# Cluster-routed attention with a SoLU feed-forward: cluster maxima in PSUM, fewer idle products, a shorter centroid norm and a new instruction order

## The chip, the cores and the metric

The kernel runs on one core of a Trainium2 chip. The metric is device time in microseconds (us) of one execution; lower is better. Five engines work side by side, each in its own program order: TensorE (PE in the profile, PEld its weight loads), VectorE (DVE), ScalarE (ACT), GpSimd (POOL) and SyncE (SP), which only issues DMAs here. They wait for each other through semaphores.

## The reference

```python
q_assign = argmax(einsum('bhsd,hcd->bhsc', q_n, c_n))     # 16 centroids a head
k_assign = argmax(einsum('bhsd,hcd->bhsc', k_n, c_n))
mask = q_assign[:, :, :, None] == k_assign[:, :, None, :]
scores = where(mask, scale * q @ k.T, -1e9)
attn = softmax(scores) @ v                                 # 4 batches, 8 heads, 768 x 64
x = attn.transpose(0, 2, 1, 3).reshape(3072, 512)
h = x @ w_in                                               # 512 -> 1024
solu = h * softmax(h)
ln = (solu - mean) / sqrt(var + 1e-6) * g_ln
return ln @ w_out                                          # 1024 -> 512, fp32
```

A query attends only to keys of its own cluster. The norm of a query or key does not change its argmax, so only the centroids are normalised.

## The kernel before, in words

The mask is made part of the score product. For every token a one-hot row of 32 values says which centroid is nearest, and it is written below the 64 rows of q and k in the operands `qbig` and `kbig`. One product over 80 or 96 rows then gives the scaled score plus a large constant where the clusters agree, and the exponential takes the constant off again, so that masked pairs come out as nothing.

The work is cut into named pieces. A table `ORDER` (names only) fixes in what order the pieces are recorded; `Weave.run` calls them one after the other, and each engine executes its own pieces in that order. A second table, `AWAY`, moves a named piece to another engine than its default. The list of needs that `add` is given (`needs`, `after`) is only checked against `ORDER`; the semaphores come from the tiles that the instructions really touch. The names used below, with the line of the profile of the kernel before:

- `S r.x` (L641): half a region of scores on TensorE, two 256-column products into a score bank pair `sb`; a region is 1024 columns. `E r` (L651): its exponential on ScalarE, 144 in all, 36 a batch.
- `V n.j` (L663): the values, six 65-column products into the one PSUM bank `ob`, of which they use the first 432 of 512 columns. `N g` (L675 reciprocal, L686 product) on VectorE normalises a group of up to six such results out of `ob`; then `ob` may be written again.
- The assignment, eleven items (`0.0`, `0.0.1`, `0.1` ... `3.2`), two pairs of heads each from batch 1 on: `cl` (L470) multiplies q and k by the centroids, `tb` (L479) transposes the result back to SBUF (`cst`), `mx` (L489) takes the maximum over the 16 centroids, `oh` (L493) compares with it and writes the one-hot rows, `ot` (L500, L505) transposes them, `pl` (L529, L531) places them in `qbig` and `kbig`. `ca` (L437, L439, L441) casts the transposed q and k, `xt` transposes them, `cv` (L554, L556) casts v.
- Batch 0 gets its q and k transposed by TensorE (`tp`, L396, fp32) with a copy out of PSUM (`xa`, `xt` with a bank, L407, L409); later batches by VectorE (L421).
- The feed-forward of 24 token tiles `f`: `h f.f2.part` (L772) and `hm` (L782), `ex` (L798), `u` (L805), `bn` (L816), `y` (L844) and its scaling `sc` (L856 on ScalarE, L858 on VectorE), `ou` the store. `wi` casts w_in (L580), `me`, `mf`, `ce` centre w_out.
- At the start, while the first DMA is under way: `wu`, idle products on TensorE (L946), and the norm of the centroids `cx`, `cy`, `cz` (L908 to L922).

The maximum lives in a small SBUF tile `mx`, and the comparison reads it broadcast over the 16 centroids:

```python
asg[t, "mx"] = pr.tile([P, 2 * HALF // NC_], F32, name="mx")
nc.vector.reduce_max(asg[t, "mx"][:, :wide(t) // NC_], each(asg[t, "cst"], t), axis=AX)
```

Of the kernel before, what the change touches and what calls it, by code (L numbers as in the profile page):

```python
# [20 lines left out]
    ca0.0.1.1.0 ca0.2.0.1 ca1.0.0.1 ca3.1.1.0 ca3.2.0.1 cv0.0.1 cv0.1.0 cv0.2.1 cv1.2.0  # L21
    cv1.3.1 cv2.0.1 cv2.1.0 cv3.0.0 cv3.0.1 cv3.3.0 pl0.0.0.1 pl0.0.1.0 pl0.1.1.1 pl2.2.1.0
    xa0.0.0 xa0.1.0 xa0.1.1 xa0.2.0 xa0.2.1 xa0.3.0 xt0.1.0 xt0.1.1 xt0.2.0 xt0.3.0
""".split(), "ACT"))
AWAY.update(dict.fromkeys("""
    as0 as11 as14 as15 as17 as18 as19 as2 as22 as23 as4 as5 as9 bl1.2 bl3.0 ce0 ce2 ce4 km mk
    pl0.0.1.0.0 pl0.1.0.0 pl0.1.0.1 pl0.2.0.0 pl0.2.1.0 pl0.3.0.0 pl0.3.1.1 pl1.0.0.0
    pl1.2.0.0 pl2.0.0.0 pl2.0.0.1 pl2.0.1.1 pl2.2.0.0 pl3.0.0.1 pl3.2.0.1 pl3.2.1.0 sc0 sc1
    sc12 sc13 sc14 sc16 sc4 sc9
""".split(), "DVE"))  # L30
AWAY.update(dict.fromkeys("""
    ca0.0.0.0.0 ca0.0.0.0.1 ca0.0.0.1.0 ca0.0.0.1.1 ce1 ce3 pl0.0.1.1 u0.0 u1.0 u10.0 u11.0
    u12.0 u13.0 u15.0 u16.0 u17.0 u18.0 u19.0 u2.0 u21.0 u22.0 u3.0 u4.0 u5.0 u6.0 u7.0 u8.0
    u9.0
# [4 lines left out]
lc ld0.0.0.0 ld0.0.1.0 ld0.0.0 ld0.0.1 ld0.1.0 ld0.1.1 lv0.0 ld0.2.0 ld0.2.1 ld0.3.0 lo3 lv0.1  # L39
ld0.3.1 lg lv0.2 lo1 lo2 lo0 cx z5 cy cz wu tp0.0.0.0 tp0.0.0.1 tp0.0.1.0 tp0.0.1.1 cp xa0.0.0  # L40
xt0.0.0 xa0.0.1 xt0.0.1 tp0.1.0.0 xa0.1.0 cb cl0.0 tb0.0 mx0.0 oh0.0 ot0.0 ca0.0.0.0.0 z3
ca0.0.1.0.0 ca0.0.0.0.1 cc ca0.0.0.1.1 ca0.0.0.1.0 pl0.0.1.1 pl0.0.0.0 ca0.0.1.0.1 ca0.0.1.1.1
ca0.0.1.1.0 tp0.1.0.1 tp0.1.1.0 xt0.1.0 xa0.1.1 cl0.0.1 tp0.1.1.1 cv0.0.1 xt0.1.1 pl0.0.0.1
tp0.2.0.0 tp0.2.0.1 tb0.0.1 mx0.0.1 oh0.0.1 ot0.0.1 pl0.0.1.0.1 pl0.0.1.0.0 pl0.0.1.1.1 cl0.1 sg
pl0.0.1.1.0 z1 ca0.1.1.0 cv0.0.0 ca0.1.0.0 xa0.2.0 pl0.0.1.0 tp0.2.1.0 xt0.2.0 xa0.2.1 S0.0 S0.1
E0 tp0.2.1.1 xt0.2.1 S1.0 tp0.3.0.0 S1.1 S2.0 S2.1 tp0.3.0.1 tb0.1 mx0.1 oh0.1 xa0.3.0 E1 E2 cl0.2
xt0.3.0 S3.0 S3.1 V0.0 V0.1 V1.0 S4.0 S4.1 V1.1 tp0.3.1.0 tb0.2 E3 S5.0 S5.1 E4 E5 ot0.1 N0 mx0.2
gt tp0.3.1.1 S6.0 S6.1 V2.0 V2.1 S7.0 S7.1 V3.0 V3.1 xa0.3.1 gk xt0.3.1 cl0.3 E6 E7 cv0.1.0
pl0.1.1.1 ca0.1.0.1 ca0.3.0.0 pl0.1.1.0 ca0.3.0.1 z2 ca0.1.1.1 oh0.2 pl0.1.0.0 pl0.1.0.1 gw S8.0
S8.1 S9.0 S9.1 me0 me1 ot0.2 tb0.3 pl0.2.1.0 N1 pl0.2.0.0 mx0.3 mk oh0.3 ca0.2.0.0 ca0.2.1.0  # L50
ca0.3.1.0 ca0.2.1.1 pl0.2.1.1 pl0.2.0.1 E8 E9 ca0.2.0.1 S10.0 S10.1 S11.0 S11.1 V4.0 V4.1 V5.0
V5.1 E10 S12.0 S12.1 cv0.2.1 E11 E12 mf N2 ot0.3 pl0.3.0.0 ld1.0.0.0 li0 ld1.0.0.1 ld1.0.0.2
ld1.0.0 ld1.0.1.0 lv0.3 ld1.0.1.1 ld1.0.1.2 ld1.0.1 cv0.1.1 ca0.3.1.1 pl0.3.1.0 pl0.3.0.1 cv0.2.0
cv0.3.0 cv0.3.1 wi0 S13.0 S13.1 V6.0 V6.1 S14.0 S14.1 V7.0 V7.1 pl0.3.1.1 N3 km ce0 E13 E14 S15.0
S15.1 S16.0 S16.1 E15 E16 V8.0 V8.1 S17.0 S17.1 E17 V9.0 V9.1 S18.0 S18.1 E18 S19.0 S19.1 N4 ce5
V10.0 V10.1 V11.0 V11.1 S20.0 S20.1 E19 S21.0 S21.1 E20 E21 li1 li3 N5 V12.0 V12.1 ptx0 S22.0
S22.1 V13.0 V13.1 li2 xt1.0.0 xt1.0.1 tx0 xt1.1.0 xt1.1.1 ld1.2.0.0 ld1.2.0.1 ld1.2.0.2 ld1.2.0
ld1.2.1.0 ld1.2.1.1 ld1.2.1.2 ld1.2.1 S23.0 S23.1 cl1.0 E22 E23 S24.0 S24.1 E24 S25.0 S25.1 E25
ca1.0.0.1 cl1.1 N6 tb1.0 tb1.1 mx1.0 ce6 ce1 ca1.0.1.0 wi1 wi3 wi2 z4 ca1.1.0.0 ca1.0.1.1
ca1.1.1.0 ca1.0.0.0 S26.0 V14.0 V14.1 S26.1 S27.0 V15.0 S27.1 V15.1 h0.0.0 h0.0.1 N7 E26 E27 S28.0  # L60
S28.1 E28 V16.0 V16.1 V17.0 S29.0 S29.1 h0.1.0 V17.1 S30.0 S30.1 E29 E30 oh1.0 hm0.0 N8 ot1.0 ce2
pl1.0.1.0 pl1.0.0.1 pl1.0.1.1 bl1.0 ce3 lv1.0 tx2 lv1.1 lv1.2 ld2.0.0.0 ld2.0.0.1 ld2.0.0.2 h0.1.1
S31.0 S31.1 V18.0 V18.1 V19.0 S32.0 S32.1 V19.1 h1.0.0 N9 hm0.1 pl1.0.0.0 xt1.2.0 E31 S33.0 S33.1
E32 E33 h1.0.1 S34.0 S34.1 V20.0 V20.1 V21.0 S35.0 S35.1 V21.1 h1.1.0 E34 E35 S36.0 S36.1 N10
hm1.0 xt1.2.1 h1.1.1 S37.0 S37.1 V22.0 V22.1 V23.0 E36 E37 S38.0 S38.1 E38 V23.1 cl1.2 N11 tb1.2
ce4 hm1.1 ex0.0 cv1.0.0 cv1.0.1 u0.0 ca1.1.0.1 S39.0 S39.1 S40.0 S40.1 V24.0 V24.1 h2.0.0 h2.0.1
V25.0 xt1.3.0 E39 E40 ex1.0 h2.1.0 h2.1.1 S41.0 S41.1 S42.0 hm2.0 h3.0.0 S42.1 V25.1 xt1.3.1 hm2.1
V26.0 V26.1 h3.0.1 E41 cl1.3 S43.0 as0 bn0.0 N12 tb1.3 mx1.2 oh1.2 bn0.1 E42 S43.1 S44.0 S44.1
V27.0 ex2.0 E43 E44 V27.1 h3.1.0 h3.1.1 V28.0 S45.0 S45.1 S46.0 S46.1 V28.1 V29.0 E45 E46 tu0
V29.1 y0.0 S47.0 S47.1 y0.1 N13 cv1.1.0 ca1.2.0.0 u1.0 ca1.2.1.0 ca1.1.1.1 cv1.1.1 ca1.3.0.1 as1  # L70
ca1.2.0.1 bn1.0 hm3.0 ot1.2 ce7 S48.0 S48.1 y0.2 V30.0 E47 E48 S49.0 S49.1 E49 tx4 ld2.0.0
ld2.0.1.0 tu1 ld2.0.1.1 ld2.0.1.2 ld2.0.1 lv1.3 ld2.2.0.0 ld2.2.0.1 ld2.2.0.2 V30.1 V31.0 V31.1
S50.0 S50.1 h4.0.0 S51.0 S51.1 E50 E51 V32.0 V32.1 y0.3 S52.0 S52.1 bn1.1 hm3.1 ag0 N14 pl1.2.0.0
pl1.2.0.1 pl1.2.1.1 pl1.2.1.0 h4.0.1 as2 bl1.2 hm4.0 ag1 al0 u2.0 ca1.2.1.1 S53.0 S53.1 V33.0
# [99 lines left out]
def kernel(  # L174
# [737 lines left out]
    def norm_2():  # L912
        nc.gpsimd.tensor_tensor(c_s0[:], c_nsq[:], halves[:, 0:1], op=Alu.pow)
# [441 lines left out]
```

## Time and profile before

| | before |
|---|---|
| time, median of 3 runs | 221.88 us (221.68 to 222.42) |
| span of the profiled execution, first to last instruction | 220.5 us |
| PE busy | 211.4 us, 96% |
| ACT busy | 192.8 us, 87% |
| DVE busy | 185.7 us, 84% |
| POOL busy | 158.8 us, 72% |
| granted TensorE clock | 1.000 |

The profiled execution has a span and no time of its own in the records; the median of the runs stands 1.4 us above its span. Busy times are sums of instruction durations; an engine's share says nothing yet of which one is waited for. In rows of groups, the columns are line, engine, operation, output <- input, partitions x elements and type, count, then busy us, mean ns of one, and the idle time just before them with what ended it. In rows of waits they are engine, tile and line, what was waited for, total us, times, longest.

### The profile page before, as it was taken

What the parts mean: (1) busy time and instruction counts of PE and PEld (TensorE: products, weight loads), DVE (VectorE), ACT (ScalarE), POOL (GpSimd) and SP (SyncE); (2) the same over time, 40 slices, a digit from 0 to 9 for tenths busy, and PEclk for the clock granted to TensorE, in tenths of its full rate; (3) what the DMA queues carried; (4) which work ended last, traced back from release to release, by engine and by line L of the source; (5) the groups of instructions that cost most, each with busy time, mean ns of one, the idle gap of its engine ahead of it and who ended that gap; (6) DMA issues with size and microseconds to landing.
All of it is one profiled execution on the core that took longest, in us unless ns stands there. A gap on an engine that the chain in (4) does not pass through costs nothing.

```text
span 220.5 us, 6292 instructions
## 1 busy us (share of the span) xinstructions
PE 211.4 (96%) x2401; PEld 148.9 (68%) x2431; DVE 185.7 (84%) x430; ACT 192.8 (87%) x245; POOL 158.8 (72%) x198
## 2 busy tenths in 40 slices
PE   7899999999999999999999999999999999999984
PEld 4567577677678776777677677666777767655442
DVE  3699979968999999896799999994888856989982
ACT  3799999999999998999999989999999888685362
POOL 3686969897898999549939997879889054456610
PEclk9999999999999999999999999999999999999999
DMA  5998999999999993999999981939584229777522
GB/s 199 394 402 259 189 175 300 126 154 259 164 154 169 190 188 62 174 248 210 153 225 162 180 184 38 171 92 209 151 173 90 72 64 168 154 120 170 163 94 100
DMA packets 120911, 38.33 MB, mean 174 GB/s; under 512 B 109993, under 2 KB 116401, under 8 KB 120881
## 3 DMA queue, kind: packets, MB, share of 16 engines
q1 hardware_dynamic: 120448, 37.40, 81.7%
q10 hardware_dynamic: 432, 0.52, 0.7%
q8 instruction: 19, 0.31, 0.6%
q14 instruction: 12, 0.09, 0.2%
HBM read 23.11 MB, written 6.29 MB: 133 GB/s over the span
## 4 chain that ended last, share of the span: by engine, by line
PE 72%; DVE 10%; DMA 6%; POOL 5%; issue 3%; ACT 2%; SPq 1%; DVEq 0%; ACTq 0%; POOLq 0%
PE sb L641 22%; PE hb L772 16%; PE mb L844 15%; PE ob L663 12%; DMA w_st<-in_moe_w_in_dram 4%; PE hb L470 3%; DMA raw<-in_q_dram 2%; DVE w_st L782 2%; PE hb L396 2%; DVE xt L421 2%; DVE bs L816 2%; POOL kbig L441 1%; PE mb L470 1%; POOL w_in_sb L580 1%; POOL v L556 1%
## 5 line engine op out<-in xcount | busy, mean ns | idle before, releaser
L651 ACT ACTIVATE e<-sb 128x1024 bf16<-128x1024 f32 x144 | 139.9, 1024 | 8.9 <-PE sb L641 8.1
L641 PE MATMUL sb<-qbig,kbig 80*128 80x256 bf16 (+3 forms) x648 | 83.8, 261 | 1.3 <-ACT e L651 1.0
L641 PEld LDWEIGHTS <-kbig 80*128 80x128 bf16 (+1 forms) x648 | 62.9, 119 | 25.4 <-issue 8.6
L805 POOL TENSOR_TENSOR u<-e_sb,w_st 128x1024 bf16<-128x1024 bf16 x21 | 45.1, 2145 | 20.0 <-ACT e_sb L798 13.3
L663 PEld LDWEIGHTS <-e 128*128 128x128 bf16 x1152 | 48.6, 97 | 10.4 <-DVE x L686 0.6
L663 PE MATMUL ob<-v,e 128*128 128x65 bf16 x1140 | 51.4, 193 | 0.2
L772 PE MATMUL hb<-w_in_sb,xT 128*128 128x512 bf16 x173 | 50.6, 379 | 0.9 <-POOL v L1323 0.3
L844 PE MATMUL mb<-w_out_c,uT 128*128 128x512 bf16 x165 | 45.5, 379 | 1.2 <-DVE y L858 0.4
L816 DVE BATCH_NORM_STATS2 bs<-u 128x6 f32<-128x512 bf16 x48 | 31.6, 680 | 1.1 <-POOL u L805 1.1
L798 ACT ACTIVATE e_sb<-w_st,nmax 128x1024 bf16<-128x1024 f32 (+1 forms) x25 | 27.8, 1113 | 3.2 <-DVE w_st L782 1.8
L439 POOL CAST qbig<-xt 64x768 bf16<-64x768 f32 (+1 forms) x31 | 25.7, 830 | 6.5 <-PE ob L663 2.7
L441 POOL TENSOR_SCALAR kbig<-xt 64x768 bf16<-64x768 f32 (+1 forms) x32 | 27.6, 865 | 2.4 <-DVE xt L409 0.8
L840 POOL TENSOR_TENSOR alpha<-var,halves 128x1 f32<-128x1 f32 x24 | 15.3, 638 | 12.6 <-DVE var L823 8.0
L421 DVE STREAM_TRANSPOSE xt<-raw 128x768 f32<-128x768 f32 x24 | 22.5, 959 | 0.1
L844 PEld LDWEIGHTS <-uT 128*128 128x128 bf16 x176 | 15.2, 97 | 10.2 <-issue 0.8
L772 PEld LDWEIGHTS <-xT 128*128 128x128 bf16 x192 | 15.8, 98 | 8.8 <-issue 0.6
L686 DVE TENSOR_TENSOR x<-ob,den 128x256 bf16<-128x256 f32 (+2 forms) x40 | 19.0, 474 | 1.4
L782 DVE TENSOR_SCALAR_CACHE_REDUCE w_st<-hb 128x512 f32<-128x512 f32 x24 | 16.3, 680 | 3.8 <-PE hb L772 3.7
L782 DVE TENSOR_SCALAR_CACHE_REDUCE w_st<-hb,nmax 128x512 f32<-128x512 f32 x24 | 17.8, 740 | 1.9 <-PE hb L772 1.5
L856 ACT ACTIVATE y<-mb,alpha 128x512 f32<-128x512 f32 x15 | 10.3, 685 | 6.5 <-POOL alpha L840 3.6
L675 DVE RECIPROCAL den<-ob 128x4 f32<-128x4 f32 (+2 forms) x40 | 7.1, 178 | 10.4 <-PE ob L663 10.1
L556 POOL CAST v<-vf 128x384 bf16<-128x384 f32 x22 | 10.9, 504 | 3.3 <-DMA vf<-in_v_dram 2.6
(109 smaller groups left out, 202.6 us busy)
## 6 DMA issues: line engine op xcount, KB each, us to landing
vf<-in_v_dram SPq DMA_DIRECT2D x16, 384.0 KB, 5.3
out_dram<-y SPq DMA_DIRECT2D x23, 256.0 KB, 2.5
raw<-in_k_dram SPq DMA_DIRECT2D x26, 192.0 KB, 4.6
raw<-in_q_dram SPq DMA_DIRECT2D x24, 192.0 KB, 5.1
w_g<-in_moe_w_out_dram SPq DMA_DIRECT2D x4, 512.0 KB, 8.7
w_st<-in_moe_w_in_dram SPq DMA_DIRECT2D x4, 512.0 KB, 8.0
raw<-in_q_dram SPq DMA_DIRECT2D x3, 384.0 KB, 6.6
raw<-in_k_dram SPq DMA_DIRECT2D x3, 384.0 KB, 7.6
```

What stands on the lines that cost most here:

```text
L421: nc.vector.transpose(xts[b, p, i][:], raw_of(b, p, i))
L439: (nc.vector if e == "DVE" else nc.gpsimd).tensor_copy(dst, src)
L441: (nc.vector if e == "DVE" else nc.gpsimd).tensor_scalar(dst, src, scalar1=inv_C, scalar2=1.0, op0=Alu.mult, op1=Alu.mult)
L641: nc.tensor.matmul(reg[:, c:c + wd], kb[u, pp, side_of(h), keys], qb[u, pp, side_of(h), su * P:su * P + wd])
L651: nc.scalar.activation(es[r][:, :w], src, Act.Exp, scale=exp_scale, bias=-exp_scale)
L663: nc.tensor.matmul(ops_of(group_of[n])[:, s, :VW], es[r][:, c0:c0 + P], v1[index[b, pair_of(h)] % R][:, side_of(h), kt, :VW], start=(kt == ...
L772: nc.tensor.matmul(hb[f2][:], xTs[f][:, dc, :], w_in_sb[:, dc, f2 * BANK:(f2 + 1) * BANK], start=(dc == 0), stop=(dc == n_dc - 1))
L782: nc.vector.tensor_scalar(ff[f, "h"][:, f2 * BANK:(f2 + 1) * BANK], hb[f2][:], scalar1=-1.0, scalar2=nmax[:, f2 - 1:f2] if f2 else 3.0e38, ...
L798: nc.scalar.activation(ff[f, "e"][:, cols(f, f2)], ff[f, "h"][:, cols(f, f2)], Act.Exp, bias=ff[f, "nmax"][:, n_ff2 - 1:], scale=-1.0, acc ...
L805: (nc.vector if e == "DVE" else nc.gpsimd).tensor_tensor(ff[f, "u"][:, cols(f, f2)], ff[f, "e"][:, cols(f, f2)], ff[f, "h"][:, cols(f, f2) ...
L816: nc.vector.bn_stats(ff[f, "bs"][:, f2, :], ff[f, "u"][:, f2 * BANK:(f2 + 1) * BANK])
L844: nc.tensor.matmul(y_of(f, x), ff[f, "uT"][:, fc, :], w_out_c[:, fc, parts_of(f, x)], start=(fc == 0), stop=(fc == n_fc - 1))
```

## The change

It has five parts.

1. The maxima are written to `ob`, columns 432 up to 480, where no value is written, in place of the SBUF tile. There is one such place, so a maximum now also comes after the comparison of the item before.
2. `wu` issues five idle products for seven. Three short ones of 256 columns, `wx0` to `wx2`, stand later: two among the transposes of batch 0, one at the very end.
3. The norm of the centroids has one VectorE instruction less; GpSimd adds the small constant instead, in a spare column of `upper`.
4. `AWAY` is new. VectorE loses the nine one-hot placings that it had from batch 1 on (seven into `qbig`, two into `kbig`), which go to GpSimd, and gains four `y` scalings from ScalarE. ScalarE loses early v casts, copies of transposes and q or k casts. GpSimd gains the nine placings, some early v casts and one step of the w_out centring, and gives up one `u` and one `wi`.
5. `ORDER` is written anew from the first name to the last.

```diff
+    def highest(t):
+        return ob[:, 6 * VS:6 * VS + wide(t) // NC_]
+
     def assign_max(t):
-        asg[t, "mx"] = pr.tile([P, 2 * HALF // NC_], F32, name="mx")
-        nc.vector.reduce_max(asg[t, "mx"][:, :wide(t) // NC_], each(asg[t, "cst"], t), axis=AX)
+        nc.vector.reduce_max(highest(t), each(asg[t, "cst"], t), axis=AX)

     def assign_hot(t):
         asg[t, "oh"] = pr.tile([P, 2 * HALF], BF16, name="oh")
         nc.vector.tensor_tensor(each(asg[t, "oh"], t), each(asg[t, "cst"], t),
-                                asg[t, "mx"][:, :wide(t) // NC_].unsqueeze(2)
+                                highest(t).unsqueeze(2)
                                 .to_broadcast([P, wide(t) // NC_, NC_]), op=Alu.is_ge)
...
     def norm_2():
         nc.gpsimd.tensor_tensor(c_s0[:], c_nsq[:], halves[:, 0:1], op=Alu.pow)
+        nc.gpsimd.tensor_scalar(c_s1[:], c_s0[:], scalar1=2e-6, scalar2=1.0, op0=Alu.add,
+                                op1=Alu.mult)

     def norm_3():
         nc.vector.reciprocal(c_r0[:], c_s0[:])
-        nc.vector.tensor_scalar(c_r0[:], c_r0[:], scalar1=c_nsq[:], scalar2=c_s0[:],
-                                op0=Alu.mult, op1=Alu.add)
-        nc.vector.tensor_scalar(c_norm[:], c_r0[:], scalar1=0.5, scalar2=1e-6,
+        nc.vector.tensor_scalar(c_norm[:], c_r0[:], scalar1=c_nsq[:], scalar2=c_s1[:],
                                 op0=Alu.mult, op1=Alu.add)
...
-        for _ in range(7):
+        for _ in range(5):
             nc.tensor.matmul(sb[0][:, 0], idle[:, :P], idle)

+    def idle_product():
+        nc.tensor.matmul(sb[0][:, 0, :2 * P], idle[:, :P], idle[:, :2 * P])
...
-        add(f"mx{tm}", "DVE", ..., tbs, [f"mx{item_name(t - 1)}"] if t else [])
+        add(f"mx{tm}", "DVE", ..., tbs + ([f"oh{item_name(t - 1)}"] if t else ["xa0.0.1"]))
...
 ORDER = """
-V41.0 V41.1 y2.0 mx2.0 as4 N17 E63 ... V42.0 V42.1 S68.0 S68.1 V43.0 V43.1 sc2 oh2.0 ot2.0 N18 pl2.0.1.1
+V41.0 V41.1 S64.1 ex4.0 y1.1 E63 mx2.0 S65.0 S65.1 y1.2 cv1.3.0 E64 N17 ... V42.0 cv1.3.1 V42.1 oh2.0 V43.0 E66
```

Two places show what moves. The first is item 2.0 of the assignment. On VectorE, before, from its maximum to its comparison and its transpose (`mx` and `cst` are SBUF tiles, `den` and `x` belong to the normalisations `N17` and `N18`):

```order
L489 TENSOR_REDUCE mx<-cst 128x48 [waits DVE_49]
L835 TENSOR_SCALAR es_1699<-esum 128x1 [waits Activation_49]
L675 RECIPROCAL den<-ob 128x6 [waits PE_49]
L686 TENSOR_TENSOR x<-ob,den 128x6x64 [waits DVE_49]
L493 TENSOR_TENSOR oh<-cst,mx 128x768
L500 STREAM_TRANSPOSE oht<-oh 128x768 [waits DVE_49]
L675 RECIPROCAL den<-ob 128x4 [waits PE_49]
```

The same stretch of VectorE after the change:

```order
L489 TENSOR_REDUCE ob<-cst 128x48 [waits DVE_49,PE_49]
L675 RECIPROCAL den<-ob 128x6 [waits DVE_49]
L686 TENSOR_TENSOR x<-ob,den 128x6x64 [waits DVE_49]
L493 TENSOR_TENSOR oh<-cst,ob 128x768 [waits PE_49]
L858 TENSOR_SCALAR y<-mb,alpha 128x512 [waits Pool_49]
L675 RECIPROCAL den<-ob 128x4 [waits PE_49]
```

The maximum and the comparison have each got a wait for TensorE that they had not: the maximum for the last product of V41.1, the comparison for the last product of V42.1, both in `ob`. The normalisation no longer waits for TensorE itself, since the maximum ahead of it has.

On TensorE after the change, the end of V42.1 and the start of V43.0 (`e` is the exponential's tile as weight, `v_1` the values):

```order
L663 LDWEIGHTS e
L663 MATMUL ob<-v_1_103,e 128x65
L663 LDWEIGHTS e
L663 MATMUL ob<-v_1_103,e 128x65
L663 LDWEIGHTS e [waits DVE_49]
L663 MATMUL ob<-v_1_103,e 128x65 [waits Pool_49]
L663 LDWEIGHTS e
```

The weight load with the wait is the first of V43.0, and the instruction that it waits for is the comparison of item 2.0. Nothing else of TensorE stands between V42.1, for which that comparison waits, and this load. In the kernel before, no wait of TensorE is for L489 or L493.

The second place is item 1.0, on VectorE after the change (`N8` is the pair with `den` and `x`):

```order
L476 STREAM_TRANSPOSE cst<-hb_93 128x384 [waits PE_49]
L489 TENSOR_REDUCE ob<-cst 128x48 [waits DVE_49,PE_49]
L675 RECIPROCAL den<-ob 128x4 [waits DVE_49]
L686 TENSOR_TENSOR x<-ob,den 128x2x2x64 [waits DVE_49]
L493 TENSOR_TENSOR oh<-cst,ob 128x768
```

and before:

```order
L479 STREAM_TRANSPOSE cst<-hb_93 128x384 [waits PE_49]
L489 TENSOR_REDUCE mx<-cst 128x48 [waits DVE_49]
L675 RECIPROCAL den<-ob 128x4 [waits PE_49]
L686 TENSOR_TENSOR x<-ob,den 128x2x2x64 [waits DVE_49]
L493 TENSOR_TENSOR oh<-cst,mx 128x768
```

After the change the maximum waits for V17.1, the normalisation and the comparison stand behind it, and V18.0 on TensorE waits for that comparison. Between V17.1 and V18.0 TensorE has S30.0, S30.1 and h0.0.0.

More of the change, by code (lines that the diff above doesn't have):

```diff
@@ L135 @@
-bn19.1 bn20.0 bn20.1 N39 hm22.0 as19 ag19 as20 as21 al19 E143 y18.0 y18.1 y18.2 y18.3 h22.1.0
-ptx23.0 h22.1.1 V95.0 ou16 sc18 V95.1 hm22.1 N40 tx23.0 ag20 tu19 y19.0 y19.1 y19.2 ptx23.1 y19.3
-tu20 ou17 tu21 ou18 ex22.0 h23.0.0 h23.1.0 tx23.1 as22 bn21.0 bn21.1 ag21 u22.0 al20 sc19 h23.0.1
-y20.0 y20.1 y20.2 y20.3 sc20 hm23.0 bn22.0 h23.1.1 ptu22.0 ptu22.1 bn22.1 hm23.1 tu22.1 tu22.0
-ex23.0 ex23.1 ou19 y21.0 y21.1 y21.2 y21.3 ou20 u23.0 u23.1 ag22 as23 ptu23.0 ptu23.1 tu23.1
-bn23.0 bn23.1 ag23 al21 sc21 ou21 tu23.0 y22.0 y22.1 y22.2 y22.3 y23.1.0 y23.1.1 y23.1.2 y23.1.3
@@ new lines @@
+V94.1 E143 h22.0.1 h22.1.0 as20 sc17 tu20 y18.0 y18.1 bn20.0 ex21.0 bn20.1 ag20 y18.2 y18.3 al18
+N39 h22.1.1 al19 sc18 ptx23.0 u21.0 hm22.0 hm22.1 V95.0 ou17 V95.1 y19.0 ou18 y19.1 al20 as21 y19.2
+N40 y19.3 ex22.0 tx23.0 h23.0.0 ptx23.1 bn21.0 h23.1.0 sc19 tx23.1 h23.0.1 h23.1.1 hm23.0 y20.0
+hm23.1 bn21.1 y20.1 y20.2 y20.3 sc20 tu21 u22.0 ex23.0 ag21 ex23.1 bn22.0 al21 ptu22.0 ptu22.1
+bn22.1 y21.0 tu22.0 tu22.1 y21.1 y21.2 as22 u23.0 y21.3 ptu23.0 as23 ou19 sc21 u23.1 bn23.0 ou20
+ptu23.1 y22.0 y22.1 y22.2 ag22 y22.3 tu23.0 tu23.1 y23.0.0 al22 y23.1.0 y23.0.1 bn23.1 y23.1.1 ag23
@@ L891 @@
     c_bd = const.tile([P, n_pair, 2 * NC_], F32, name="c_bd")
[L894 removed]
+    upper = const.tile([P, 120], F32, name="upper")
+    upper, c_s1 = upper[:, :2], upper[:, 2:3]
     nc.gpsimd.memset(upper[:], 0.0)
```

218 lines of the change are left out of this document (108 added, 110 removed).

## The prediction

> **What bounds the kernel now.** I read the page's busy times first, then its time slices, then each engine's busy time in stretches of the span, then the list of waits, and the timeline at the places of the change.
>
> ```profile
> PE 211.4 (96%) x2401; PEld 148.9 (68%) x2431; DVE 185.7 (84%) x430; ACT 192.8 (87%) x245; POOL 158.8 (72%) x198
> PEclk9999999999999999999999999999999999999999
> ```
>
> TensorE is busy 96% of the span, at the full granted clock in every slice. The span is 220.5 us, so what can be gained without taking work from TensorE is 220.5 - 211.4 = 9.1 us and no more. The stretches say where that idle time lies; the columns are the stretch, its length, then busy time of PE, PEld, DVE, ACT and POOL.
>
> ```profile
> 0.00:10.00 10.00, 8.34 (x48) 4.81 (x48) 4.21 (x19) 4.94 (x10) 4.74 (x21) 1.00 0.79 285
> ...
> 10.00:50.00 40.00, 38.26 (x499) 27.40 (x501) 34.90 (x75) 39.02 (x49) 33.01 (x47) 1.00 1.01 233
> 50.00:85.00 35.00, 34.73 (x435) 26.11 (x436) 33.33 (x73) 34.34 (x42) 31.22 (x35) 1.00 1.02 178
> 90.00:200.00 110.00, 108.93 (x1267) 78.14 (x1285) 93.02 (x218) 100.13 (x125) 76.54 (x82) 1.00 0.79 151
> 210.00:215.00 5.00, 4.39 (x32) 2.19 (x31) 4.37 (x13) 3.76 (x8) 0.55 (x1) 1.00 0.28 102
> 5.57:28.69 23.12, 22.04 (x244) 14.44 (x243) 20.00 (x47) 21.26 (x33) 18.06 (x34) 1.00 0.99 300
> ```
>
> From 10 to 50 us TensorE idles 1.74 us, and there ScalarE is busy 39.02 of 40: batch 0 runs at ScalarE's pace. From 50 to 85 and from 90 to 200 us TensorE idles 0.27 + 1.07 us in 145. There it is the bound: what ScalarE, VectorE or GpSimd save is worth nothing, and a stall of TensorE is lost. In the tail, from 210 to 215, it idles 0.61. The waits show how little TensorE stands for the other engines, and that VectorE stands for TensorE's values.
>
> ```profile
> PE sb L641 <- ACT e L651: 1.0, 3, 0.3
> PEld L663 <- DVE x L686: 0.6, 1, 0.6
> PE mb L844 <- DVE y L858: 0.4, 1, 0.4
> ...
> DVE den L675 <- PE ob L663: 10.1, 17, 1.3
> ```
>
> **Part one: batch 0 under other engines and another order, a gain.** The tables take from ScalarE, among the exponentials of batch 0, copies of transposes, v casts and casts of q or k.
>
> ```profile
> 12.99 1.02 ACT L651 ACTIVATE e<-sb 128x1024 bf16<-128x1024 f32 x1
> 28.45 2.85 ACT L651 ACTIVATE e<-sb 128x1024 bf16<-128x1024 f32 x3
> 39.10 1.94 ACT L651 ACTIVATE e<-sb 128x1024 bf16<-128x1024 f32 x2 [0.19 <-PE sb L641]
> L407 ACT COPY xt<-hb 128x384 f32<-128x384 f32 x11 | 5.2, 481 | 2.7 <-PE hb L396 2.5
> L554 ACT CAST v<-vf 128x384 bf16<-128x384 f32 x10 | 5.1, 512 | 0.1
> L556 POOL CAST v<-vf 128x384 bf16<-128x384 f32 x22 | 10.9, 504 | 3.3 <-DMA vf<-in_v_dram 2.6
> L531 POOL COPY kbig<-oht 32x384 f32<-32x384 f32 x3 | 1.5, 504 | 0.2
> ```
>
> Three exponentials back to back take 2.85 us and one 1.02, so they follow each other by (2.85 - 1.02) / 2 = 0.92. The first starts at 12.99, the 26th at 39.10 + 0.92 = 40.02: 27.03 us for 25 steps, which alone need 23.0. The other 4.0 us is ScalarE's further work and its waits. By the new table one copy (0.48) and one placing of about the same length stay of it, so ScalarE could gain 3.1. GpSimd takes over part of that work, and could have become the limit: up to the last pair's key placing, which ends at 28.69, it is busy 18.06 of 23.12 us, and gets four v casts and two placings of 0.504 more, less a short one of about 0.3. That is 18.06 + 2.7 = 20.8, an end at 26.3 at best, 2.4 us earlier than now. TensorE's own idle time, 1.74 and the 0.47 that the first row leaves behind its first product at 1.19 us, comes to 2.2, and since a pipelined product's busy time covers part of its neighbour's, a little more is there. Between 2.2 and 3.1 I take **-2.6**, near the two lower figures, with 0 and -3.1 as bounds. Those early comparisons that make TensorE wait, three in batch 0, are inside this term, since they eat the same idle time.
>
> The shorter norm and the idle products lie in that start. The removed step is one instruction of VectorE ahead of the first transposed centroids, the added one stands on GpSimd beside it, and five idle products end earlier than seven by two of them, which the transposes behind can use only once their q has landed. I count these at nothing, and up to +1.2 if the clock opens late.
>
> ```profile
> 1.19 3.17 PE L946 MATMUL sb<-w_in_sb 128*128 128x512 bf16 x7 [1.19 <-DVE halves L884]
> 4.15 1.48 PE L396 MATMUL hb<-ident_f,raw 128*128 128x128 f32 x6
> 8.29 0.87 PE L396 MATMUL hb<-ident_f,raw 128*128 128x128 f32 x6
> ```
>
> Six transposes took 1.48 us at 4.15 and 0.87 at 8.29, so a dozen that run late at the slow rate cost 1.2. On this the Trainium skill (TensorE: Matmul & The Clock Gate, Part 1) says that the clock doubles after some 3.4 us of sustained work, and the rows agree, as the work began at 1.19; the new fillers among the transposes keep that work going.
>
> **Part two: the tail and one stall, a gain.** In the new order `y20` stands behind `h23.1.1`, so that the last token tile's own chain (`hm23`, `ex23`, `u23`, its transposes, `y23`) starts four products sooner, and those four fill its waits. What they can fill is the 0.61 us of 210 to 215: **-0.6**, from 0. The one wait of `y` for VectorE's scaling, 0.4 in the list above, is placed otherwise: **-0.3**, from 0.
>
> **Part three: maxima in the bank of the values, a loss.** `ob` is one tile, so its writers and readers take turns. The order rows show the turns: the maximum waits for the values ahead of it, the comparison for those between, the next values for the comparison. Before, only the normalisation stood between two groups of values.
>
> ```profile
> L489 DVE TENSOR_REDUCE mx<-cst 128x48 f32<-128x768 f32 x6 | 5.7, 948 | 0.1
> L493 DVE TENSOR_TENSOR oh<-cst,mx 128x768 bf16<-128x768 f32 x6 | 7.2, 1206 | 0.0
> L479 DVE STREAM_TRANSPOSE cst<-hb 128x384 f32<-128x384 f32 x12 | 6.8, 577 | 0.5 <-PE hb L470 0.2
> L675 DVE RECIPROCAL den<-ob 128x6 f32<-128x6 f32 x16 | 3.0, 185 | 2.4 <-PE ob L663 2.3
> L686 DVE TENSOR_TENSOR x<-ob,den 128x256 bf16<-128x256 f32 x23 | 9.8, 424 | 0.8
> L686 DVE TENSOR_TENSOR x<-ob,den 128x384 bf16<-128x384 f32 x16 | 8.9, 557 | 0.6
> L663 PE MATMUL ob<-v,e 128*128 128x65 bf16 x1140 | 51.4, 193 | 0.2
> 42.65 0.95 DVE L493 TENSOR_TENSOR oh<-cst,mx 128x768 bf16<-128x768 f32 x1
> 62.58 1.55 DVE L493 TENSOR_TENSOR oh<-cst,mx 128x768 bf16<-128x768 f32 x1
> 62.50 2.32 POOL L441 TENSOR_SCALAR kbig<-xt 64x768 bf16<-64x768 f32 x2
> 102.71 0.81 PE L772 MATMUL hb<-w_in_sb,xT 128*128 128x512 bf16 x3
> 103.36 1.04 PE L641 MATMUL sb<-qbig,kbig 96*128 96x256 bf16 x8
> 104.23 0.60 PE L772 MATMUL hb<-w_in_sb,xT 128*128 128x512 bf16 x2
> ```
>
> The cover, in starts: three products of `h` from 102.71 to 103.36 are 0.65, so a part of two is 0.43; two whole regions of scores from 103.36 to 104.23 are 0.87, so one is 0.435. A turn costs the last value's product (0.19), the VectorE work, and the way back to TensorE, which I put at 0.05. For the comparison I take 0.95, its time alone; it took 1.55 when GpSimd's casts had begun 0.08 us before it. Place by place, each with TensorE's work in between:
>
> - 1.0: maximum 0.95, normalisation 0.18 + 0.42, comparison 0.95, with 0.24 around them 2.74; cover S30 and h0.0.0, 0.87. Stall 1.9.
> - 1.2: from the last centroid product transpose 0.58, maximum 0.95, normalisation 0.19 + 0.56, a small instruction of 0.15, comparison 0.95, with 0.24 around them 3.6, and five hand-overs inside VectorE of about 0.05, 3.9; cover three regions and three parts of `h`, 2.6. Stall 1.3.
> - 2.0: comparison with no cover at all, 0.19 + 0.95 + 0.05. Stall 1.2.
> - 2.2: maximum 1.2 between V53.0 and V53.1; cover S82 and h8.1.0, 0.87. Stall 0.3.
> - 3.0: comparison 1.2 between V61.0 and V61.1; cover h10.1.0, 0.43. Stall 0.8.
> - 3.2: work enough in between, none.
>
> That is 5.5, of which I take off 0.5 at 1.0, where TensorE idles in part anyway for ScalarE (the 1.0 us of waits for `sb`): **+5.0**. Bounds are 0, if VectorE's work is already covered, and 6.8, if the comparison keeps its mean of 1.21 at the five places. Queued behind the waiting maximum and comparison on VectorE are the normalisations and the `y` scalings; who waits for these is again TensorE.
>
> The Trainium skill bears on this twice. PSUM — Partial Sum Buffer, PSUM bank collisions raise a hardware error, says that two engines must not touch one bank in the same partitions at once, disjoint columns included; if columns alone counted, this term would be 0. The built order agrees with the page, as the waits are there though the columns are apart. SBUF — State Buffer, SBUF: two separate sides, says that a VectorE operation with two SBUF inputs and GpSimd lock each other out of a shared port pair; the comparisons of 0.95 and 1.55 agree. By that the comparison, with one input now in PSUM, always takes the short time, which speaks for the change.
>
> **Sum.** Span 220.5 - 2.6 - 0.6 - 0.3 + 5.0 = 222.0. The median of the runs stands 221.88 - 220.5 = 1.4 above the span, so 223.4. The other moves, nine placings from VectorE to GpSimd and four scalings from ScalarE to VectorE, lie in the stretch that TensorE bounds, at nothing.
>
> **Rivals.** *The waits are covered* (faster): TensorE's queue takes up work early enough, or VectorE is ahead, and a third of the stalls remains, 1.6. Then 221.9 - 3.5 + 1.6 = 220.0. For it: VectorE is busy only 93 of 110 us from 90 to 200, and the gains are in stretches with real idle time. Against it: at 2.0 there is no instruction between. *The turns spread* (slower still): VectorE, itself standing for values (10.1 us already), falls behind at each turn, its normalisations come late and GpSimd, with ten us more to do, places late; 2 us on top of the sum, 225.4. It decides if VectorE's idle time before its reads of `ob` grows beyond 15 us. *Both sides cancel*: batch 0 gives 3.1 and the stalls 3.3, or less of each, 221.8. *The change does not do what it says*, the waits being there and the early gains not: 221.9 + 5.0 = 226.9.
>
> **Chances.** The forecast 0.42, covered waits 0.30, spread 0.12, cancelled 0.12, no early gain 0.04. Its range reaches from the covered case, with 0.6 below it, to beyond the spread one: 219.4 to 226.2. About 0.3% (0.67 us) is what a measurement can tell here. Faster by more than that, 0.31 (the covered case and a little of the forecast's lower end); within it 0.13; slower 0.56.
>
> **What would show it.** In the changed trace: the 16th exponential starts 2 us or more earlier than 30.28 (part one); TensorE's waits for L489 and L493 appear by name, some 5 us in five or six places, the longest about 1.9 at item 1.0; the comparisons all take near 0.95; TensorE idles under 0.3 from 210 to 215 less its shift. Wrong would be: waits for L493 of less than 2 us in all (the covered case), or TensorE's busy time itself longer, which nothing here foresees.

## The result, and the profile after

The kernel after takes 236.59 us, the median of 4 runs (236.0 to 237.91), against 222.15 for the kernel before in the same set; the ratio is 1.065, with a 95% interval of 1.061 to 1.069. The prediction was 223.4 with a range up to 226.2: the direction was right and the size far too small. The span of the profiled execution is 234.2 us, 13.7 above that of before. The granted clock stayed open in two of the four executions (236.0 and 236.39) and closed for a while in the other two (236.8 and 237.91); what that costs is taken up below.

The page's busy times and granted clock after, then the same stretches as in the prediction:

```profile
PE 214.1 (91%) x2398; PEld 147.2 (63%) x2432; DVE 189.1 (81%) x426; ACT 189.3 (81%) x234; POOL 162.7 (69%) x214
PEclk9999999999999999999999999999999999999999
```

```profile
10.00:50.00 40.00, 33.43 (x439) 23.07 (x438) 33.88 (x67) 32.86 (x38) 30.63 (x46) 1.00 1.06 244
50.00:85.00 35.00, 33.95 (x424) 25.61 (x425) 29.98 (x66) 33.09 (x38) 31.91 (x37) 1.00 0.81 138
90.00:200.00 110.00, 104.58 (x1207) 74.58 (x1226) 88.21 (x198) 95.61 (x116) 76.20 (x87) 1.00 0.73 143
210.00:215.00 5.00, 5.00 (x35) 2.65 (x35) 4.81 (x15) 3.58 (x6) 2.85 (x3) 1.00 0.90 234
```

TensorE's idle time from 10 to 50 us rose from 1.74 to 6.57 us, and ScalarE, busy 39.02 of these 40 before, is now busy 32.86: batch 0 no longer runs at ScalarE's pace, and it is not faster. From 90 to 200 idle time rose from 1.07 to 5.42. Over the span TensorE's idle time is up by 11.0 us and its busy time by 2.7; the prediction had named longer busy time as a sign of being wrong. The clock stayed at full in this execution. TensorE waits for VectorE at these places (timeline of TensorE, the rows of which the releaser is VectorE, from 20 us on; two of 0.23 and 0.15 near the end are left out):

```profile
20.71 0.34 PE L663 MATMUL ob<-v,e 128*128 128x65 bf16 x6 [0.65 <-DVE ob L489]
26.77 0.38 PE L641 MATMUL sb<-qbig,kbig 80*128 80x256 bf16 x2 [0.62 <-DVE qbig L531]
45.87 0.53 PE L663 MATMUL ob<-v,e 128*128 128x65 bf16 x12 [1.88 <-DVE x L686]
49.78 0.34 PE L663 MATMUL ob<-v,e 128*128 128x65 bf16 x6 [1.93 <-DVE oh L493]
71.17 0.35 PE L663 MATMUL ob<-v,e 128*128 128x65 bf16 x6 [0.67 <-DVE oh L493]
94.48 0.54 PE L663 MATMUL ob<-v,e 128*128 128x65 bf16 x12 [1.05 <-DVE oh L493]
114.57 0.34 PE L663 MATMUL ob<-v,e 128*128 128x65 bf16 x6 [0.38 <-DVE ob L489]
132.51 0.34 PE L663 MATMUL ob<-v,e 128*128 128x65 bf16 x6 [0.61 <-DVE oh L493]
136.43 0.34 PE L663 MATMUL ob<-v,e 128*128 128x65 bf16 x6 [0.59 <-DVE x L686]
176.74 0.65 PE L641 MATMUL sb<-qbig,kbig 80*128 80x128 bf16 x8 [0.83 <-DVE kbig L543]
```

Six rows name the maximum (L489) or the comparison (L493): 5.29 us in all, at the items that the prediction lists, and one in batch 0. The others are no turns of the bank, though two hang on turns: with the maxima in SBUF (the first experiment below) the wait at 136.43 is not there and that at 26.77 is 0.32. The row at 45.87, 1.88 us, is a normalisation that came late, and VectorE's timeline says why:

```profile
41.78 1.26 DVE L580 CAST w_in_sb<-w_st 128x1024 bf16<-128x1024 f32 x1
...
42.97 2.30 DVE L618 SCALAR_TENSOR_TENSOR w_out_c<-w_g,g_ln,y 128x512 bf16<-128x512 f32 x1
...
45.18 0.17 DVE L675 RECIPROCAL den<-ob 128x4 f32<-128x4 f32 x1
45.39 0.42 DVE L686 TENSOR_TENSOR x<-ob,den 128x256 bf16<-128x256 f32 x1
```

A cast of w_in and a centring of w_out, weight work, stand ahead of the normalisation N7 in VectorE's order, and V16.0 waits for N7. The row at 176.74 is the zeroing L543 (`bl3.2`): the new table gives it to VectorE, where it waits 2.67 us for scores that still read the old `kbig`, and then TensorE waits for it.

### The profile page after: what moved, and what is told of

Read it like the earlier page. It is cut to its first block, busy times and chain, and to the rows that moved or that the text cites. A ratio compares the mean times of both kernels' runs of the same rounds, so it can differ in the third digit from the quotient of the medians.

```text
span 234.2 us, 6291 instructions
## 1 busy us (share of the span) xinstructions
PE 214.1 (91%) x2398; PEld 147.2 (63%) x2432; DVE 189.1 (81%) x426; ACT 189.3 (81%) x234; POOL 162.7 (69%) x214
## 4 chain that ended last, share of the span: by engine, by line
PE 74%; DVE 17%; issue 3%; DMA 3%; ACT 2%; DVEq 0%; ACTq 0%
PE sb L641 24%; PE hb L772 15%; PE mb L844 14%; PE ob L663 13%; PE hb L467 4%; ACT e L651 2%; PE hb L393 2%; DMA xT<-x 2%; DVE bs L816 2%; DVE oh L493 2%; DVE w_st L782 1%; DVE ob L489 1%; DVE u L805 1%; DMA c_all<-in_centroids_dram 1%; DVE w_out_c L618 1%
## 5 line engine op out<-in xcount | busy, mean ns | idle before, releaser
L651 ACT ACTIVATE e<-sb 128x1024 bf16<-128x1024 f32 x144 | 142.2, 1022 | 24.0 <-PE sb L641 21.7
L641 PE MATMUL sb<-qbig,kbig 80*128 80x256 bf16 (+3 forms) x648 | 93.8, 262 | 3.0 <-DVE kbig L543 0.8
L641 PEld LDWEIGHTS <-kbig 80*128 80x128 bf16 (+1 forms) x648 | 61.5, 121 | 30.6 <-issue 12.0
L663 PEld LDWEIGHTS <-e 128*128 128x128 bf16 x1152 | 51.6, 97 | 23.1 <-issue 7.8
L663 PE MATMUL ob<-v,e 128*128 128x65 bf16 x1140 | 55.9, 193 | 8.3 <-DVE oh L493 4.3
L772 PE MATMUL hb<-w_in_sb,xT 128*128 128x512 bf16 x174 | 51.7, 379 | 1.4 <-DMA xT<-x 0.7
L805 POOL TENSOR_TENSOR u<-e_sb,w_st 128x1024 bf16<-128x1024 bf16 (+1 forms) x20 | 41.9, 2095 | 13.5 <-ACT e_sb L798 12.8
L840 POOL TENSOR_TENSOR alpha<-var,halves 128x1 f32<-128x1 f32 x24 | 13.1, 548 | 22.4 <-DVE var L823 21.7
L531 POOL COPY kbig<-oht 32x768 f32<-32x768 f32 (+2 forms) x18 | 12.8, 713 | 13.4 <-DVE oht L500 9.9
L772 PEld LDWEIGHTS <-xT 128*128 128x128 bf16 x192 | 16.8, 98 | 6.8 <-DMA xT<-x 0.8
L675 DVE RECIPROCAL den<-ob 128x4 f32<-128x4 f32 (+2 forms) x40 | 7.1, 178 | 12.4 <-PE ob L663 11.9
L856 ACT ACTIVATE y<-mb,alpha 128x512 f32<-128x512 f32 x11 | 7.5, 685 | 9.0 <-PE mb L844 8.9
```

The costliest lines, as they stand in the source:

```text
L641: nc.tensor.matmul(reg[:, c:c + wd], kb[u, pp, side_of(h), keys], qb[u, pp, side_of(h), su * P:su * P + wd])
L651: nc.scalar.activation(es[r][:, :w], src, Act.Exp, scale=exp_scale, bias=-exp_scale)
L663: nc.tensor.matmul(ops_of(group_of[n])[:, s, :VW], es[r][:, c0:c0 + P], v1[index[b, pair_of(h)] % R][:, side_of(h), kt, :VW], start=(kt == ...
L772: nc.tensor.matmul(hb[f2][:], xTs[f][:, dc, :], w_in_sb[:, dc, f2 * BANK:(f2 + 1) * BANK], start=(dc == 0), stop=(dc == n_dc - 1))
L805: (nc.vector if e == "DVE" else nc.gpsimd).tensor_tensor(ff[f, "u"][:, cols(f, f2)], ff[f, "e"][:, cols(f, f2)], ff[f, "h"][:, cols(f, f2) ...
```

## The experiments

Three theories stood at the start. A: the turns in `ob` make nearly all of the loss. B: turns make about half, and the new order with its engines the other half, through queues on VectorE and GpSimd. C: the turns only stand where something else would be waited for next. Where a ledger is named below, it is TensorE's idle time worked out from the traces: the gaps between the starts of its products beyond their usual spacing, laid side by side at equal work done. No view prints it. It gives 9.2 us for before and 22.9 for after, and their difference, 13.7, is that of the spans. A stall by the ledger is 0.1 to 0.2 longer than its row in the timeline.

**One thing undone, one thing done alone.** The first kernel is after with the maxima in the SBUF tile again:

```diff
-        nc.vector.reduce_max(highest(t), each(asg[t, "cst"], t), axis=AX)
+        asg[t, "mx"] = pr.tile([P, 2 * HALF // NC_], F32, name="mx")
+        nc.vector.reduce_max(asg[t, "mx"][:, :wide(t) // NC_], each(asg[t, "cst"], t), axis=AX)
...
-                                highest(t).unsqueeze(2)
+                                asg[t, "mx"][:, :wide(t) // NC_].unsqueeze(2)
```

> The kernel after the change with one thing undone: the maxima are in the SBUF tile mx again; order, engines, idle products and norm are those of after. Theory A, turns in the bank ob make nearly all of the loss: TensorE's waits for L489 and L493 in the trace after add up to 4.3 + 2.3 + 1.0 = 7.6 us by name, and what follows from them makes up the rest, so the time falls from 236.6 to 225 or below. Theory B, turns are about half and the new order with its engines makes the other half through queues on VectorE: 236.6 - 7 = 229 to 231. Theory C, the turns only stand where something else would be waited for next: 234 or more.

Measured: 231.68 us (229.91 to 232.44), ratio 1.042 (1.036 to 1.048). The turns cost 4.9 us in this order by the medians: nearest theory B, which ended at 231. Theory A and theory C fall. The medians mix executions with the clock open and closed: here it closed in three of four. At an open clock it is 236.0 and 236.39 against 229.91, some 6.3 us, though the last is one execution; with one closing each it is 236.8 and 237.91 against 231.63 to 232.44, some 5.6. By the medians 9.5 us are left to find.

The second is the opposite edit on the kernel before.

> The kernel before with one thing done: the maxima are in ob; order, engines, idle products and norm are those of before. In its order the comparison often stands right behind the maximum or next to a normalisation, so fewer turns are new. Theory A and theory B with the same price a turn: by the built waits seven places in which TensorE waits for a maximum or a comparison, some 0.5 us each beyond the normalisation, +2 to +4, 224 to 226. Theory C: 221.5 to 223.

Measured: 238.96 us (237.44 to 239.41), ratio 1.075 (1.071 to 1.080). All expectations were wrong: the same edit costs 16.8 us in the order of before. There the turns are fewer and longer. TensorE's timeline in this kernel, where lines are three higher (L492 is the maximum, L496 the comparison, L666 the values):

```profile
27.08 1.48 PE L666 MATMUL ob<-v,e 128*128 128x65 bf16 x24 [2.15 <-DVE oh L496]
...
44.83 0.52 PE L666 MATMUL ob<-v,e 128*128 128x65 bf16 x12 [1.38 <-DVE ob L492]
...
68.50 0.54 PE L666 MATMUL ob<-v,e 128*128 128x65 bf16 x12 [1.69 <-DVE oh L496]
...
121.79 0.34 PE L666 MATMUL ob<-v,e 128*128 128x65 bf16 x6 [2.20 <-DVE oh L496]
```

These are 7.4 us; in the order of after such waits are 0.38 to 1.93. Most of the rest of the 16.8 follows from them: four late normalisations (2.5 us), one late step of the feed-forward (1.7), and the granted clock, which closes twice in this trace and in three of the four executions (0.986), by an estimate from 3.4 us of half speed each time another 3.4. So the price belongs to order and bank together. That it is set by what TensorE has to do between the two groups of values is read from the order and not tested.

**Order and engines crossed.** Two kernels with maxima in SBUF take one table from each side: the whole of `ORDER` from one kernel, the whole of `AWAY` from the other.

> The order of after, but the table of engines of before, and the maxima in SBUF; norm and idle products of after. Against the first run of this set it differs in the engines alone. If the order is what costs beside the turns: within 2 us of that run. If the engines cost (w_in cast and w_out centring on VectorE ahead of a normalisation, placings on GpSimd): 4 us or more below it, near 223.

> The kernel before with the table of engines of after; order, maxima in SBUF, norm and idle products of before. If the engines cost: 226 or more. If the order costs: 221 to 224.

Measured: 237.61 us (235.72 to 238.23) for the order of after with the engines of before, where a fourth execution at a granted clock of 0.971 took 240.74, and 251.71 (249.41 to 252.66) for the order of before with the engines of after. With both tables of one side it is 222.15 and 231.68. The first lies outside both theories; the second keeps the letter of "226 or more" and is far beyond it: the two tables do not add. Pieces that move to other engines without new places in those engines' order cost far more (29.6 us) than the prediction's "nothing". Part of that is again the clock: 0.973 in the trace, which is some 13.5 of 250.6 us at half speed, or by an estimate 7 us.

**Single entries of the tables put right.** From here on the base is the first kernel, and each run adds to the one before it, the two runs on the kernel before aside. A warning holds for all of these: the first score starts between 12.16 and 14.14 us in their traces, by when the first q lands, so a single step of about 1 us is at the limit of what the medians tell. First:

```diff
-V15.1 ce0 ce2 E26 N7
+V15.1 N7 ce0 ce2 E26
```

> The kernel after with the maxima in SBUF, and one entry of the order moved: N7 stands ahead of ce0 and ce2 on VectorE. In the first run of this study TensorE stood 2.06 us for that normalisation, which had two centrings of w_out (2.29 us) ahead of it, and 1.8 us later the granted clock was 0.50 for 3.4 us. Theory A (order on VectorE plus clock): both go, so the time falls by 2 for the stall and by about 1.6 for the clock, to 228 from 231.7. Theory B (the wait only moves to what is next): 231 or more.

Measured: 230.38 us (229.18 to 231.5), 1.3 less by the medians, where theory A had 3.6 and theory B under 0.7. The granted clock stays at full in its trace. The stall of 2.06 us for N7 is gone, and one of 1.32 stands at the next normalisation, N8, which has the centring ahead of it now. So more than half of the wait moved. The intervals of the two ratios overlap (1.0361 to 1.0482 and 1.0314 to 1.0385), and the one execution of the first kernel with an open clock, 229.91, is no slower than this: what is gained by the medians can be the clock alone, which closes in none of these six executions.

```diff
-AWAY: bl3.2 on VectorE, u23.0 on GpSimd
+      bl3.2 on GpSimd, u23.0 on VectorE (the defaults)
```

> As the run before, and two table entries undone: the zeroing bl3.2 (L543 of after) is on GpSimd again, the first half of u23 on VectorE again. In the trace of after TensorE stood 0.99 us at 176 for that zeroing, which waited for the scores ahead of it, and in the tail 0.63 + 0.49 + 0.32. Theory A: 1.0 less for the zeroing and 0.3 to 0.5 less for the tail, 226.5 to 227. Theory B: within 0.5 of the run before.

Measured: 229.08 us (228.67 to 231.05), 1.3 less. The size is near theory A's, but the cause is not: the stall before these scores is 0.64 in place of 0.77, so the zeroing itself is late on GpSimd too, and TensorE's two waits for `u23` are 0.51 us in all, where they were 0.48. The two traces differ in the first score, which starts at 12.16 in place of 14.14, since q landed sooner in the one. With ratio intervals that overlap (1.0275 to 1.0351), a gain from these two entries is not shown.

> The kernel before with five idle products for seven and the shorter norm; order, engines and maxima as before, no short fillers. By the prediction worth nothing, up to +1.2 if the clock opens late: 222 to 223. If the new start is what costs the first 1.5 us of the kernel after, 223.5 or more. A gain would show the first score earlier than 12.35 by 0.3 or more and the time at 221.7 or less.

> The kernel before with one entry of the order moved: h23.1.1 ahead of y20. By the prediction's part two the last tile's chain starts four products sooner and they fill TensorE's 0.6 us of idle time between 210 and 215: 221.5 to 221.7. If the tail is bound otherwise: 222.1 or more.

The kernel before with five idle products and the shorter norm: 222.51 us against 222.31, ratio 1.000 (0.998 to 1.003). With h23.1.1 ahead of y20: 222.32, ratio 1.000 (0.998 to 1.001). Both are no change. In the trace of the first the first score starts 0.7 us later than before (13.02 for 12.35) and the span is 0.3 longer (220.8 for 220.5), so part of a small delay in the start is taken up later. In the second, the tail's idle time stayed at 0.9 to 1.1 in the ledger, since the chain behind the last tile ends as late as before.

```diff
-V15.1 N7 ce0 ce2 E26 ... oh1.0 E29
+V15.1 N7 E26 ... oh1.0 ce0 ce2 E29
-AWAY: pl1.2.0.0 on GpSimd
+      pl1.2.0.0 on VectorE (as before)
```

> As e6, and two more entries undone or moved: the placing pl1.2.0.0 is on VectorE again as before (in e6 TensorE stood 1.09 us at 75 for it, queued on GpSimd behind a cast), and the w_out centring ce0, ce2 stands behind the comparison oh1.0 on VectorE (in e6 TensorE stood 1.31 us at 46 for the normalisation N8 behind it). Theory A, each of these queues is a loss by itself: 229.1 - 1.1 - 1.2 = 226.8. Theory B, the waits only move: 228.5 or more.

Measured: 227.89 us (227.35 to 228.94), 1.2 less, of 2.3 expected. The placing's wait shows in the first kernel of the study (timeline, lines three lower than in after):

```profile
76.83 0.82 POOL L436 CAST qbig<-xt 64x768 bf16<-64x768 f32 x1
...
77.69 0.82 POOL L528 COPY qbig<-oht 32x768 f32<-32x768 f32 x1
...
78.56 0.60 PE L638 MATMUL sb<-qbig,kbig 80*128 80x256 bf16 x4 [0.94 <-POOL qbig L528]
```

The placing is one of the nine that left VectorE (eight went to GpSimd, one to ScalarE, and GpSimd took another from ScalarE); on GpSimd a cast for later stands ahead of it. Put back, it ended that wait and the centring's 1.3 went, but forty products later TensorE now stands 0.65 us for a normalisation on VectorE, at 78.33, where it had not stood: the waits go in part and move in part.

```diff
-ca0.1.0.0 pl0.0.1.1 cl0.1 pl0.0.1.1.1
+pl0.0.1.1 cl0.1 pl0.0.1.1.1 ca0.1.0.0
```

> As the run before, and in batch 0 one cast on GpSimd (ca0.1.0.0, 0.82 us) stands behind a placing instead of ahead of it. In the trace of after, that cast starts at 10.14 and VectorE's placing of 192 columns, begun at 10.26, takes 0.81 us where its like take 0.25 to 0.29; the rest of the chain to the first score stands behind it. If the two engines hold each other up: that placing takes under 0.35, the first score comes 0.4 us or more earlier, the time 0 to 0.5 lower. If not: the placing stays near 0.8.

Measured: 227.11 us (226.67 to 228.23), 0.8 less by the medians, though the intervals of the two ratios overlap (1.0207 to 1.0274 before the move, 1.0176 to 1.0238 behind it). VectorE's placing in the two traces, ahead of the move with the cast beside it and behind the move without:

```profile
11.11 0.83 POOL L436 CAST qbig<-xt 64x768 bf16<-64x768 f32 x1
11.29 0.77 DVE L528 COPY kbig<-oht 32x192 f32<-32x192 f32 x1
```

```profile
11.06 0.25 DVE L528 COPY kbig<-oht 32x192 f32<-32x192 f32 x1
```

The placing took 0.77 us beside the cast, which began first and ended 0.12 before it, and 0.25 alone; the cast took no longer than its like (0.82). So the cast holds up the placing, by 0.5 us, and in batch 0 that is on the path to the first score, which starts at 12.41 in place of 13.16 (some 0.2 of that is a sooner q). On this the Trainium skill (SBUF — State Buffer, SBUF: two separate sides) has VectorE, in some of its instructions, and GpSimd share a port pair that the one which starts first holds for its whole instruction; the two durations agree.

> As the first run of this set, with the maxima in ob as in after. If turns are a price by themselves, as in after against the first run of the study (4.9 us): 4 to 6 above the first run of this set. If they were only as dear because other things were late too: under 3 above it.

Measured: 234.83 us (233.91 to 236.38), 6.9 above its like with the maxima in SBUF. Turns are a price by themselves, somewhat above the 4 to 6 expected, and not cheaper with the queues repaired. In its trace the granted clock closes once as well, at 0.50 to 0.67 from 48 to 52 us, as in two of the six executions. The four with an open clock have a median of 234.3, 6.4 above the like, so at an open clock the price is much the same in both orders: 6.3 and 6.4.

> The first kernel of the study once more, for a second trace. There TensorE idled from 44.0 to 46.0 and the granted clock was 0.50 from 48 to 51. If an idle stretch of 2 us always closes the clock, the same drop is there again; if it depends on where the stretch falls, it may be absent, and the span is 1.5 us shorter.

One execution: 232.43 us, span 230.7 against 229.9. The clock closed again. Stretches of the two traces of that one kernel, the first trace, then this one, and then the trace of after; the columns are the stretch, its length, busy times by engine (TensorE first), and behind them the granted clock:

```profile
44.00:46.00 2.00, 0.11 (x2) 0.01 (x1) 1.97 (x4) 1.04 (x2) 2.00 (x2) 1.00 1.11 177
...
44.21:47.62 3.41, 1.64 (x33) 1.53 (x33) 3.31 (x7) 1.58 (x2) 1.85 (x2) 1.00 1.14 183
47.62:51.03 3.41, 3.41 (x35) 2.47 (x33) 2.40 (x4) 2.39 (x3) 0.89 (x2) 0.50 1.05 215
```

```profile
42.72:46.14 3.42, 1.55 (x25) 0.86 (x18) 3.37 (x5) 2.05 (x3) 3.05 (x3) 1.00 1.14 181
46.14:49.55 3.41, 3.41 (x32) 2.40 (x29) 2.62 (x5) 1.94 (x2) 0.00 (x0) 0.50 1.04 190
```

```profile
41.61:45.03 3.42, 2.37 (x25) 1.20 (x23) 3.42 (x3) 3.25 (x4) 3.42 (x4) 1.00 1.11 177
45.03:48.44 3.41, 1.99 (x33) 1.70 (x34) 2.38 (x6) 1.59 (x3) 0.91 (x1) 1.00 1.18 187
48.44:51.85 3.41, 2.07 (x35) 1.73 (x35) 2.87 (x5) 1.61 (x3) 0.83 (x2) 1.00 1.03 211
```

A stall of 1.9 us at the same place closed the clock for 3.4 us both times, once from 47.6 and once from 46.1. In the trace of after, the same stall and another of 1.9 behind it (45.87 and 49.78) left the clock open. So it depends on when the stall falls, and the traces' records of the clock say how. It opens at 6.66 us in the first trace, at 5.18 in the second and at 4.07 in after. Both closings come 40.96 us behind that, which is twelve times 3.413, and last 3.413. Counted in such stretches from the opening, as the rows above are, TensorE is busy for 1.64 and 1.55 us in the stretch ahead of a closing. In after the two stalls are split by the edges, and none of the three stretches is under 1.99. In all fourteen traces, up to the last product, a stretch with over 1.7 us of idle time has a closing behind it, and one with under 1.4 has none; between these both occur. This rule is fitted to the traces and no run was made to test it; in one trace the clock also stayed closed for two stretches. By an estimate from 3.4 us at half speed a closing costs 1.7 us; the first kernel takes 229.91 without one and 231.63 to 232.44 with one.

## Why the prediction was right and wrong

**Part three, the turns: right.** It gave +5.0; undone in after, the turns are worth 4.9 by the medians and some 6.3 at an open clock. By place it had 1.9, 1.3, 1.2, 0.3 and 0.8; the named waits are 1.93, 0.67, 1.05, 0.38 and 0.61. The comparison takes 948 ns on the mean of six in after and took 1206 before, as expected of the short time. That the bank does this, and not the order, shows in the second kernel of the study, which keeps the order of before; the row of after, then of that kernel:

```profile
L493 DVE TENSOR_TENSOR oh<-cst,ob 128x768 bf16<-128x768 f32 x6 | 5.7, 948 | 2.6 <-PE ob L663 2.6
...
L496 DVE TENSOR_TENSOR oh<-cst,ob 128x768 bf16<-128x768 f32 x6 | 5.7, 952 | 6.3 <-PE ob L666 6.3
```

In the order of after it was 994 in SBUF already, so there the bank gave little of it.

**Part one, batch 0: nothing gained.** It gave -2.6 and the 16th exponential 2 us earlier. These are ScalarE's rows of the 15th and 16th exponential, and of the 35th and 36th, the last of batch 0; first before, then after, then the kernel with the maxima in SBUF and all moves of the study (`e10_after_more2_lock`):

```profile
29.36 1.95 ACT L651 ACTIVATE e<-sb 128x1024 bf16<-128x1024 f32 x2
49.81 1.96 ACT L651 ACTIVATE e<-sb 128x1024 bf16<-128x1024 f32 x2
...
30.18 1.94 ACT L651 ACTIVATE e<-sb 128x1024 bf16<-128x1024 f32 x2
53.57 2.01 ACT L651 ACTIVATE e<-sb 128x1024 bf16<-128x1024 f32 x2
...
30.11 1.94 ACT L648 ACTIVATE e<-sb 128x1024 bf16<-128x1024 f32 x2
49.84 2.01 ACT L648 ACTIVATE e<-sb 128x1024 bf16<-128x1024 f32 x2
```

In after the 15th starts 0.8 us later and the 35th 3.8. Without the turns and with the queues put right, the 35th starts when it did before: the term is 0 at best, not -2.6.

The step that failed is the reading that ScalarE, busy 39.02 of 40 us, sets the pace, so that work taken from it shortens the stretch. ScalarE was busy 6.2 us less from 10 to 50 us, some 4 of it because only 31 exponentials fell there in place of 35, and then waited for scores (21.7 us over the span, 8.1 before). Its next limit was close behind: by the rows, scores wait for placings on ScalarE, VectorE and GpSimd (0.87, 0.32 and 0.32 us in the first kernel of the study), and a placing on VectorE takes longer beside a cast (0.77 for 0.25). I had bounded the gain by GpSimd's sum of work, which left out the order of its queue and what its work does to VectorE's. That these waits are the limit is read from the rows; no run takes them all away.

**"The other moves, at nothing": the largest error.** The moves lie in the stretch that TensorE bounds, and I took that for cover. But a moved piece stands in some engine's order ahead of other work, and where TensorE waits for that work, a stretch that TensorE bounds is no cover. Order, engines, norm and idle products were to give -3.5 in all, and without the turns they cost 9.5. With the maxima in SBUF, six moves brought 231.68 to 227.11, 4.6 us, which is clear of the noise though most single steps are not. Some 1.8 of it, from 231.68 to 229.91, is the clock; the rest is the stalls for N7, N8 and the placing and the 0.5 us ahead of the first score, less what moved. What stays, 4.7 us against the kernel before, is in the ledger as waits of under 1 us each: some 2 in the first work of TensorE, part of it idle products that are no longer issued (the first score starts no later, 12.41 for 12.35), 1.0 in batch 0, 0.9 at the normalisation behind the placing, 0.75 at the zeroing, 0.3 late in the feed-forward and 0.7 in the tail, less 1.0 that it gains between 25 and 45 us. These were read from the ledger and not undone, and the part in the start varies by 1 us from trace to trace, so the last 4.7 us are placed by about 1 us and their cause stays open.

**Part two, the tail: nothing.** It gave -0.6 and -0.3; the tail alone on the kernel before is 1.000. The wait of 0.4 for VectorE's scaling is not among after's waits, but one for ScalarE's scaling grew from 0.25 to 0.47, and no run tries that term alone. In after `u23.0` on GpSimd also stands in the tail's chain, which I had not counted; put back, it changed nothing there.

**The rivals.** The one without early gains (226.9, chance 0.04) named the right failure and had no room for the moves; none ended above 227. The spreading turns (225.4) came near their sign: VectorE stood 11.9 us before its reciprocals and 2.8 before its comparisons, 14.7 of the 15 asked for, and the normalisation at 136.43 is late by a turn. The covered case at 0.30 is out: 5.29 us of named waits. Of "what would show it", the waits of L493 and L489 came as forecast, the exponential did not, and TensorE's idle time from 210 to 215 is 0 with the tail elsewhere.

No version here beats the kernel before: undoing all that was undone still leaves 227.11.

## What to carry to other kernels

An order and its table of engines are one object: crossed, the two tables cost some 30 and 15 us over the kernel before, where the other pair costs 9.5, so a new table is costed by walking each engine's queue to the next instruction that the bound engine waits for, not by summing what each engine gains. A scratch value in a bank that a loop writes can cost a turn at each use, and what covers a turn is what the bound engine has to do in between; count it place by place, as that was the term that came out right. A busy share near 100% in a stretch names the present limit, not the gain: ask how far behind the next one is before counting work taken off it.

## What the hardware showed that was not expected

A stall of TensorE of 1.9 us can halve the granted clock afterwards, for 3.4 us, and need not: it did so in two of three traces with that stall, and where it fell in the clock's stretches of 3.41 us tells which. On this the Trainium skill (TensorE: Matmul & The Clock Gate, Part 1) puts an idle window of about 3.4 us ahead of the closing; here 1.8 and 1.9 us without a product in a stretch of 3.41 were enough. And a small VectorE copy took three times its time (0.77 for 0.25) beside a GpSimd cast. A centring took 2.30 us in after, at 42.97, with these GpSimd operations beside it, where the five of before averaged 0.83 (timeline of after, group of before); that GpSimd is the cause is read from the rows and was not tried alone:

```profile
42.46 1.27 POOL L438 TENSOR_SCALAR kbig<-xt 64x768 bf16<-64x768 f32 x1
43.68 1.03 POOL L580 CAST w_in_sb<-w_st 128x1024 bf16<-128x1024 f32 x1
44.66 1.28 POOL L436 CAST qbig<-xt 64x768 bf16<-64x768 f32 x1
```

```profile
L618 DVE SCALAR_TENSOR_TENSOR w_out_c<-w_g,g_ln,y 128x512 bf16<-128x512 f32 x5 | 4.1, 830 | 0.0
```
